# A three-stage kernel on one core: list masks from 16-bit pairs, softmax sums in groups of five tiles, V spread on GpSimd

## The chip, the cores and the metric

The kernel runs on one core of one Trainium2 chip. The metric is the device time of one execution in microseconds. Five engines work beside each other, each through its own queue in order: TensorE (PE; its weight loads are listed as PEld), VectorE (DVE), ScalarE (ACT), GpSimd (POOL) and SyncE (SP, which only issues transfers).

## The reference, cut to what matters

Three stages follow each other: attention over pooled keys and values, a mixture of experts with the best two of eight, and a dense two-layer block.

```
# attention: B, H, S, D = 8, 8, 576, 64; keys and values are means over 8 rows
k_p = k.reshape(B, H, Sp, 8, D).mean(axis=3);  v_p = v.reshape(B, H, Sp, 8, D).mean(axis=3)
scores = 1/sqrt(D) * q @ k_p.T
attn = exp(scores - max);  attn /= attn.sum + 1e-9
x = (attn @ v_p).transpose(0, 2, 1, 3).reshape(4608, 512)
# experts: N, D, E, F = 4608, 512, 8, 1024
logits = x @ w_gate + log1p(exp(x @ w_noise)) * noise
top2 = the two largest of 8;  w = softmax over the two
out[t] = sum over its two experts of w * (relu(x[t] @ w1[e]) @ w2[e])
# dense block: 512 -> 2048 -> 512
h = x @ w_in;  result = (h - tanh(h)) @ w_out
```

## The kernel before, in words

**Attention** (function attention) walks over 36 tiles of 128 tokens. It is a software pipeline written out by hand: in step t of one loop the exponentials of tile t stand beside the matmuls of its neighbours. In the order of one step: ACT does the exponentials of tile t (st_exps) and copies x transposed of tile t-4 (st_xT); DVE does the softmax sum of tile t-1 (st_norm: add 1e-9, reciprocal) and the scaled output of tile t-6 (st_g: the rows xr, which go to memory, and the gate logits lg); PE transposes the attention weights of tile t-2 (st_attT) and q of tile t+2 (st_q), multiplies the scores of tile t+1 (st_scores, after which DVE takes the row maximum mx), multiplies the output of tile t-5 with the identity and the gate weights (st_x, into px, of which there is one buffer), and attention weights by V of tile t-3 (st_av). px of one tile can be written only when xr and lg of the tile before have been read out of it.

Each of the 8 batches (4.5 tiles) has its K and V loaded, summed over the 8 rows of a pool in three halvings (the first on GpSimd for batches from 2 on, five instructions each for K and V; the other two on VectorE), and spread. For V this is vscale: VectorE computes a power of two from the largest value (lines 101 to 103), a scaled mask of8 (L1261), and in one instruction of 1280 elements per partition VB, the V of all heads set apart from each other (L1262). VB has two buffers, for even and odd batches. st_av of the batch's first tile stands one step later.

**The gate** (gate_jobs, lists) works on groups of 10, 10, 9 and 7 tiles as soon as their logits are there. It is a Python generator: each yield is a place where the loop may go on with other work. tick(n) takes n such pieces; a step of the loop has a fixed number of ticks, between its own instructions, so that the gate's small VectorE instructions stand spread between those of attention. What PE has to multiply is held until the next tick_pe. After the last tile, six more steps empty the pipeline (a step then ends in eight ticks), and what is left of the gate is taken in the first units of the first expert.

The lists say which tokens go to which expert's slot. For up to five tiles at a time, lists builds 0/1 masks and multiplies them on PE: l_one is 1 where the slot number k (of 80) equals a token's column, l_col holds that mask times the tile's first token number (head) and, by ACT, times the lane; l_row is 1 where k (of 128) equals a token's row. Before, l_one and l_col are one VectorE instruction of 800 elements each (L1465, L1466), and l_row is one instruction of 256 elements per tile (L1470), each with its own tick. Columns, rows and head are 32-bit numbers with one value per token, read with a stride of zero; the slot numbers and the masks are 16-bit.

**Experts and dense block.** When the second group is done, its lists give the tokens of expert 0's first 512 rows, which POOL gathers (L1587) and PE transposes (L1598). moe then runs 24 groups of tokens through two matmul layers (L355 to L357, L377 to L379), in single 16-bit halves; the dense block follows. PSUM of attention is given back before the experts' first product (L355) starts.

Of the kernel before, what the change touches and what calls it, by code (L numbers as in the profile page):

```python
# [10 lines left out]
F32 = mybir.dt.float32  # L11
F16 = mybir.dt.float16
BF16 = mybir.dt.bfloat16
I32 = mybir.dt.int32
# [1095 lines left out]
def attention(nc, tc, st, V):  # L1110
# [104 lines left out]
    nz = ep.tile([128, NT, E], F32, name="nz")  # L1215
    for c in each:
        add(nc.vector, 0, "k", 4, slice(*c))
    head = ep.tile([128, NT], F32, name="head")
    nc.gpsimd.iota(head, pattern=[[128, NT]], base=0, channel_multiplier=0, allow_small_or_imprecise_dtypes=True)
    zero8 = ep.tile([128, 1, E], F32, name="zero8")  # L1220
    nc.vector.memset(zero8, 0.0)
    dd = ep.tile([128, NT], F32, name="dd")
# [3 lines left out]
    def prep_jobs(b, first=False):  # L1226
        tl = {}
# [26 lines left out]
        def vscale():  # L1254
            p = ps.tile([128, 1], F32, name="pt", bufs=4)
            nc.tensor.matmul(p, ones1, tl["vx"], start=True, stop=True)
            yield
            m = wk.tile([128, 3], F32, name="vs")
            pow2(nc, m, p)
            of8 = wk.tile([128, 5, 4], F32, name="of8")  # L1260
            ts(of8, of, m[:, 2:3], None, op0=OP.mult)  # L1261
            tt(VB[b % 2].rearrange("p c (j d) -> p c j d", d=D), tl["va"][:, :, 0:1].to_broadcast([128, 5, 4, D]),  # L1262
               of8[:, :, :, None].to_broadcast([128, 5, 4, D]), op=OP.mult)
            lo, hi = b * S, b * S + S
            t0, t1 = lo // 128, -(-hi // 128)
            for t in range(t0, t1):
                o0, o1 = max(lo - 128 * t, 0), min(hi - 128 * t, 128)
                if o1 - o0 < 128:
                    ts(isc[o0:o1, t:t + 1], m[o0:o1, 1:2], 1.0 / 128, None, op0=OP.mult)
            f0, f1 = -(-lo // 128), hi // 128  # L1270
            ts(isc[:, f0:f1], m[:, 1:2].to_broadcast([128, f1 - f0]), 1.0 / 128, None, op0=OP.mult)
# [35 lines left out]

    def st_exps(t):
        at = wk.tile([128, 2, 4, SP], F32, name="at", bufs=3)
        sm = wk.tile([128, 2, 4], F32, name="sm", bufs=3)  # L1310
        AT[t], SM[t] = at, sm
        for g, (p, mx) in enumerate(SC.pop(t)):
            for j in range(4):
                nc.scalar.activation(at[:, g, j], p[:, j], AF.Exp, bias=mx[:, j:j + 1], accum_out=sm[:, g, j:j + 1])  # L1314

    def st_norm(t):
        sm = SM.pop(t)
        ts(sm, sm, 1e-9, None, op0=OP.add)
        tick()
        rc = RC[t] = wk.tile([128, H], F32, name="rc", bufs=7)  # L1320
        nc.vector.reciprocal(rc, sm.rearrange("p a b -> p (a b)"))
        tick()

    def st_attT(t):
# [67 lines left out]
    def gate_jobs(t0, n):  # L1392
# [5 lines left out]
        def T(nm, shp=None, d=F32):  # L1398
            tl[nm] = ep.tile([128, n] + (shp or [E]), d, name="g_" + nm, bufs=1)
            return tl[nm]  # L1400
# [40 lines left out]
            nc.vector.tensor_reduce(sp, tl["oh"], axis=AX.X, op=OP.add)  # L1441
        yield
        spf = sp.rearrange("p t a o -> p t (a o)")
        hi, row = T("hi", [2], I32), T("row", [2])
        yield ts(hi, spf, 7, None, op0=OP.logical_shift_right)
        yield stt(row, hi, -128.0, spf, op0=OP.mult, op1=OP.add)
        yield tt(tl["e"], tl["e"], hi, op=OP.add)
        over = T("ov", [2])
        yield ts(over, hi, float(NB), 1000.0, op0=OP.is_ge, op1=OP.mult)
        yield tt(tl["e"], tl["e"], over, op=OP.add)  # L1450
        yield from lists(t0, n, row, tl["e"])

    def lists(t0, n, row, col):


        K = E * NB
        flat = idx[:, :, 0:NB]
        for c0 in range(0, n, LT):
            m = min(LT, n - c0)
            R = ep.tile([128, LT, 2, 128], F16, name="l_row", bufs=1)[:, 0:m]  # L1460
            C0 = ep.tile([128, LT, 2, K], F16, name="l_one", bufs=1)[:, 0:m]
            C = ep.tile([128, LT, 2, 2, K], F16, name="l_col", bufs=1)[:, 0:m]
            b = lambda a, k: a[:, c0:c0 + m, :, None].to_broadcast([128, m, 2, k])
            w = lambda k: slot[:, None, None, 0:k].to_broadcast([128, m, 2, k])
            yield tt(C0, w(K), b(col, K), op=OP.is_equal)  # L1465
            tt(C[:, :, :, 1], C0, head[:, t0 + c0:t0 + c0 + m, None, None].to_broadcast([128, m, 2, K]),  # L1466
                                    op=OP.mult)
            yield nc.scalar.activation(C[:, :, :, 0], C0, AF.Copy, scale=lane)
            for j in range(m):
                yield tt(R[:, j], w(128)[:, j], b(row, 128)[:, j], op=OP.is_equal)  # L1470
            yield "pe"
            p = gate_ps[-1]([128, 2, E, NB])
            for j in range(m):
                for a in range(2):
                    nc.tensor.matmul(p.rearrange("p x e c -> p (x e c)"), R[:, j, a], C[:, j, a].rearrange("p x k -> p (x k)"),
                                     start=(j + a == 0), stop=(j == m - 1 and a == 1))
            yield 2 * (now[0] < NT)
            yield tt(flat, p[:, 0], flat, op=OP.add)
            yield tt(flat, p[:, 1], flat, op=OP.add)
# [241 lines left out]
```

## Time and profile before

| what | value |
|---|---|
| time, median of 3 runs | 1829.58 us (1828.01 to 1830.68) |
| the profiled execution | 1828.06 us, span 1826.2 us |
| PE busy in the span | 1763.6 us (97%) |
| DVE, ACT, POOL busy | 1301.2, 940.9, 263.2 us |
| mean granted clock of TensorE | 0.992 |

The profile's second part cuts the span into 40 slices of 45.7 us and gives the busy share of each engine in tenths. Attention takes the first six. From slice 7 on PE stands at 9 nearly throughout; in slices 1 and 4 to 6 it stands at 7 to 8, and the granted clock (PEclk) falls to 8 in slice 6:

```
PE   7998889999999999999999999999999999999998
DVE  5788867776676667566566456687878879787775
PEclk8999989999999999999999999999999999999999
```

(The slices are counted from 1 here. The lines are those of the page.)

### The profile page before, as it was taken

The page shows a single profiled execution, that of the slowest core. Times are in us where ns is not written, and L with a number is a line of the kernel's source. Part 1 is how long each engine was busy: PE and PEld are TensorE (multiplying, and loading weights), DVE is VectorE, ACT ScalarE, POOL GpSimd, SP SyncE. Part 2 cuts the span into 40 slices and gives each one's busy share as a digit, 9 for nine tenths or more (in the row PEclk, how much of TensorE's full clock was granted, in tenths as well). Part 3 has the DMA queues.
Part 4 walks back from the last instruction along what each step waited for, and adds up shares of the span by engine and source line. Part 5 has one row for each costly group of instructions (what it writes and reads, how often), then busy time and mean ns, then how long its engine had stood idle before and what let it go on. Part 6 is the DMA issues. An engine that isn't in the chain of part 4 may idle for free. (4 is left out here: it accounts for less than half of the span.)

```text
span 1826.2 us, 28991 instructions
## 1 busy us (share of the span) xinstructions
PE 1763.6 (97%) x10791; PEld 1077.7 (59%) x10792; DVE 1301.2 (71%) x2640; ACT 940.9 (52%) x2249; POOL 263.2 (14%) x258
## 2 busy tenths in 40 slices
PE   7998889999999999999999999999999999999998
PEld 5998874445445454545445454566666666666664
DVE  5788867776676667566566456687878879787775
ACT  5886732443434343443424245565766657666554
POOL 2222001312113030110101012110111201010000
PEclk8999989999999999999999999999999999999999
DMA  9867223464464545454544434531313313041100
GB/s 224 236 166 205 61 74 108 141 161 130 141 187 122 183 129 165 139 147 124 146 106 121 103 110 120 118 89 34 93 38 74 83 42 91 24 93 46 37 24 25
DMA packets 264158, 203.45 MB, mean 111 GB/s; under 512 B 188160, under 2 KB 208640, under 8 KB 264000
## 3 DMA queue, kind: packets, MB, share of 16 engines
q1 hardware_dynamic: 251840, 162.16, 33.0%
q0 software_dynamic: 11904, 38.81, 8.2%
q8 instruction: 88, 1.44, 0.3%
q14 instruction: 70, 0.57, 0.1%
q10 hardware_dynamic: 256, 0.46, 0.1%
HBM read 121.82 MB, written 45.74 MB: 92 GB/s over the span
## 5 line engine op out<-in xcount | busy, mean ns | idle before, releaser
L359 ACT ACTIVATE hT<-ph 128x512 f16<-128x512 f32 (+2 forms) x192 | 96.8, 505 | 425.0 <-PE ph L357 418.8
L355 PE MATMUL ph<-xTp,pair 128*128 128x384 f16 (+2 forms) x736 | 245.2, 333 | 14.0 <-DMA xTp<-xp 4.8
L356 PE MATMUL ph<-xTp,pair 128*128 128x384 f16 (+2 forms) x736 | 244.9, 333 | 0.4 <-DVE xTp L336 0.4
L357 PE MATMUL ph<-xTp,pair 128*128 128x384 f16 (+2 forms) x736 | 244.9, 333 | 0.0
L360 DVE SCALAR_TENSOR_TENSOR hT<-ph,hT 128x512 f16<-128x512 f32 (+2 forms) x192 | 110.8, 577 | 163.3 <-ACT hT L359 161.5
L1042 PE MATMUL py<-wo,gT 128*128 128x512 f16 x576 | 218.3, 379 | 1.0 <-issue 1.0
L1040 PE MATMUL py<-wo,gT 128*128 128x512 f16 x576 | 218.3, 379 | 0.1
L377 PE MATMUL py<-pair,hT 128*128 128x512 f16 x576 | 218.3, 379 | 0.0
L378 PE MATMUL py<-pair,hT 128*128 128x512 f16 x576 | 218.3, 379 | 0.0
L379 PE MATMUL py<-pair,hT 128*128 128x512 f16 x576 | 218.3, 379 | 0.0
L1041 PE MATMUL py<-wo,gT 128*128 128x512 f16 x576 | 218.3, 379 | 0.0
L899 PEld LDWEIGHTS <-wi 128*128 128x128 f16 x1536 | 150.3, 98 | 58.5 <-issue 0.2
L315 POOL DMA_INDIRECT xg<-x_d,idx x75 | 85.5, 1139 | 669.8 <-DVE xp L342 462.3
L713 POOL DMA_INDIRECT y<-y_d,ridx x64 | 78.9, 1233 | 518.5 <-DVE y L724 240.7
L355 PEld LDWEIGHTS <-pair 128*128 128x128 f16 x768 | 75.0, 98 | 83.6 <-issue 24.9
L356 PEld LDWEIGHTS <-pair 128*128 128x128 f16 x768 | 75.1, 98 | 61.8 <-issue 6.0
L357 PEld LDWEIGHTS <-pair 128*128 128x128 f16 x768 | 75.1, 98 | 57.1 <-issue 0.6
L999 ACT ACTIVATE th<-th,bias 128x512 f32<-128x512 f32 x144 | 102.5, 712 | 3.3 <-DVE th L997 1.6
L1000 DVE SCALAR_TENSOR_TENSOR th<-th,t 128x512 f32<-128x512 f32 x144 | 98.6, 684 | 1.4 <-ACT th L999 1.4
L989 DVE TENSOR_TENSOR gT<-th,gT 128x512 f16<-128x512 f32 x144 | 98.7, 685 | 0.2 <-ACT gT L988 0.2
L996 DVE SCALAR_TENSOR_TENSOR t<-hb,cinf,hs 128x512 f32<-128x512 f32 x64 | 48.0, 749 | 70.9 <-ACT hs L995 68.8
L1314 ACT ACTIVATE at<-psc,mx 128x72 f32<-128x72 f32 x288 | 87.8, 334 | 18.6 <-DVE mx L1303 18.6
(305 smaller groups left out, 3496.6 us busy)
## 6 DMA issues: line engine op xcount, KB each, us to landing
stage<-in_moe_w SPq DMA_DIRECT2D x64, 512.0 KB
y_d<-ys SPq DMA_DIRECT2D x82, 256.0 KB
x_d<-xr SPq DMA_DIRECT2D x36, 256.0 KB
out<-o SPq DMA_DIRECT2D x36, 256.0 KB
qt<-in_q SPq DMA_DIRECT2D x32, 256.0 KB
raw<-in_moe_w_in SPq DMA_DIRECT2D x32, 256.0 KB
raw<-in_moe_w_out SPq DMA_DIRECT2D x32, 256.0 KB
kt<-in_k SPq DMA_DIRECT2D x7, 768.0 KB
```

What stands on the lines that cost most here:

```text
L355: nc.tensor.matmul(p[:, :nt], w[:, 0, m, s], x[:, 0, m, :nt], start=(m == 0), stop=False)
L356: nc.tensor.matmul(p[:, :nt], w[:, 0, m, s], x[:, 1, m, :nt], start=False, stop=False)
L357: nc.tensor.matmul(p[:, :nt], w[:, 1, m, s], x[:, 0, m, :nt], start=False, stop=(m == KD - 1))
L360: stt(h[:, 1, :nt], p[:, :nt], 0.0, h[:, 0, :nt], op0=OP.max, op1=OP.subtract)
L377: nc.tensor.matmul(p, h[:, 0, s], w[:, 0, f], start=(f == 0), stop=False)
L378: nc.tensor.matmul(p, h[:, 0, s], w[:, 1, f], start=False, stop=False)
L379: nc.tensor.matmul(p, h[:, 1, s], w[:, 0, f], start=False, stop=(f == KF - 1))
L899: nc.tensor.matmul(p, w[:, a, m], y[:, c, b, m], start=(start and m + x == 0), stop=(m == 1 and x == 2), skip_group_check=True)
L999: nc.scalar.activation(q, q, AF.Square, bias=bias[:, 2:3], scale=SP5)
L1040: nc.tensor.matmul(p, g[:, 0, s], wo[:, 0, f], start=(f == 0), stop=False)
L1041: nc.tensor.matmul(p, g[:, 0, s], wo[:, 1, f], start=False, stop=False)
L1042: nc.tensor.matmul(p, g[:, 1, s], wo[:, 0, f], start=False, stop=(f == KF - 1))
```

## The change

Four things are changed, all in attention.

- **Masks in pairs.** row, col and head become 16-bit, and each value is stored twice side by side (a last dimension of 2). The three mask operations read pairs, so that every operand of theirs is 16-bit with two neighbours in its innermost dimension. The sum e + over is written straight into the pairs of col.
- **Row masks as one operation.** l_row of up to five tiles is one instruction of 1280 elements, and so one tick where there were five.
- **Softmax sums per five tiles.** The exponentials' sums are gathered for five tiles (the groups that the tuple sums marks: five tiles, twice four or less). The addition of 1e-9 and the reciprocal are done once for the group, after its last tile; in the other steps their two ticks are taken without them.
- **V on GpSimd.** For batches from 2 on, the instruction that writes VB is issued on GpSimd. For batches 0 and 1 it stays on VectorE.

```diff
@@ -1215,8 +1215,8 @@
     nz = ep.tile([128, NT, E], F32, name="nz")
     for c in each:
         add(nc.vector, 0, "k", 4, slice(*c))
-    head = ep.tile([128, NT], F32, name="head")
-    nc.gpsimd.iota(head, pattern=[[128, NT]], base=0, channel_multiplier=0, allow_small_or_imprecise_dtypes=True)
+    head = ep.tile([128, NT, 2, 2], F16, name="head")
+    nc.gpsimd.iota(head, pattern=[[128, NT], [0, 4]], base=0, channel_multiplier=0, allow_small_or_imprecise_dtypes=True)
     zero8 = ep.tile([128, 1, E], F32, name="zero8")
     nc.vector.memset(zero8, 0.0)
     dd = ep.tile([128, NT], F32, name="dd")
@@ -1259,7 +1259,7 @@
             pow2(nc, m, p)
             of8 = wk.tile([128, 5, 4], F32, name="of8")
             ts(of8, of, m[:, 2:3], None, op0=OP.mult)
-            tt(VB[b % 2].rearrange("p c (j d) -> p c j d", d=D), tl["va"][:, :, 0:1].to_broadcast([128, 5, 4, D]),
+            (nc.gpsimd if b > 1 else nc.vector).tensor_tensor(VB[b % 2].rearrange("p c (j d) -> p c j d", d=D), tl["va"][:, :, 0:1].to_broadcast([128, 5, 4, D]),
                of8[:, :, :, None].to_broadcast([128, 5, 4, D]), op=OP.mult)
             lo, hi = b * S, b * S + S
             t0, t1 = lo // 128, -(-hi // 128)
@@ -1307,18 +1307,28 @@
 
     def st_exps(t):
         at = wk.tile([128, 2, 4, SP], F32, name="at", bufs=3)
-        sm = wk.tile([128, 2, 4], F32, name="sm", bufs=3)
-        AT[t], SM[t] = at, sm
+        if t in sums:
+            SM[0] = wk.tile([128, 5, 2, 4], F32, name="sm"), t
+        sm, t0 = SM[0]
+        AT[t] = at
         for g, (p, mx) in enumerate(SC.pop(t)):
             for j in range(4):
-                nc.scalar.activation(at[:, g, j], p[:, j], AF.Exp, bias=mx[:, j:j + 1], accum_out=sm[:, g, j:j + 1])
+                nc.scalar.activation(at[:, g, j], p[:, j], AF.Exp, bias=mx[:, j:j + 1], accum_out=sm[:, t - t0, g, j:j + 1])
+        if t + 1 in sums or t + 1 == NT:
+            SM[1] = sm, t0
 
     def st_norm(t):
-        sm = SM.pop(t)
+        if not (t + 1 in sums or t + 1 == NT):
+            tick(2)
+            return
+        sm, t0 = SM.pop(1)
+        sm = sm[:, 0:t + 1 - t0]
         ts(sm, sm, 1e-9, None, op0=OP.add)
         tick()
-        rc = RC[t] = wk.tile([128, H], F32, name="rc", bufs=7)
-        nc.vector.reciprocal(rc, sm.rearrange("p a b -> p (a b)"))
+        rc = wk.tile([128, 5, H], F32, name="rc")[:, 0:t + 1 - t0]
+        nc.vector.reciprocal(rc, sm.rearrange("p t a b -> p t (a b)"))
+        for u in range(t0, t + 1):
+            RC[u] = rc[:, u - t0]
         tick()
 
     def st_attT(t):
@@ -1441,14 +1451,15 @@
             nc.vector.tensor_reduce(sp, tl["oh"], axis=AX.X, op=OP.add)
         yield
         spf = sp.rearrange("p t a o -> p t (a o)")
-        hi, row = T("hi", [2], I32), T("row", [2])
+        hi, row, col = T("hi", [2], I32), T("row", [2, 2], F16), T("col", [2, 2], F16)
+        two = lambda a: a[:, :, :, None].to_broadcast([128, n, 2, 2])
         yield ts(hi, spf, 7, None, op0=OP.logical_shift_right)
-        yield stt(row, hi, -128.0, spf, op0=OP.mult, op1=OP.add)
+        yield stt(row, two(hi), -128.0, two(spf), op0=OP.mult, op1=OP.add)
         yield tt(tl["e"], tl["e"], hi, op=OP.add)
         over = T("ov", [2])
         yield ts(over, hi, float(NB), 1000.0, op0=OP.is_ge, op1=OP.mult)
-        yield tt(tl["e"], tl["e"], over, op=OP.add)
-        yield from lists(t0, n, row, tl["e"])
+        yield tt(col, two(tl["e"]), two(over), op=OP.add)
+        yield from lists(t0, n, row, col)
 
     def lists(t0, n, row, col):
 
@@ -1460,14 +1471,13 @@
             R = ep.tile([128, LT, 2, 128], F16, name="l_row", bufs=1)[:, 0:m]
             C0 = ep.tile([128, LT, 2, K], F16, name="l_one", bufs=1)[:, 0:m]
             C = ep.tile([128, LT, 2, 2, K], F16, name="l_col", bufs=1)[:, 0:m]
-            b = lambda a, k: a[:, c0:c0 + m, :, None].to_broadcast([128, m, 2, k])
-            w = lambda k: slot[:, None, None, 0:k].to_broadcast([128, m, 2, k])
-            yield tt(C0, w(K), b(col, K), op=OP.is_equal)
-            tt(C[:, :, :, 1], C0, head[:, t0 + c0:t0 + c0 + m, None, None].to_broadcast([128, m, 2, K]),
-                                    op=OP.mult)
+            g = lambda a: a.rearrange("p t a (k i) -> p (t a) k i", i=2)
+            b = lambda a, t, k: a[:, t:t + m].rearrange("p t a i -> p (t a) i")[:, :, None].to_broadcast([128, 2 * m, k // 2, 2])
+            w = lambda k: slot[:, None, 0:k].to_broadcast([128, 2 * m, k]).rearrange("p m (k i) -> p m k i", i=2)
+            yield tt(g(C0), w(K), b(col, c0, K), op=OP.is_equal)
+            tt(g(C[:, :, :, 1]), g(C0), b(head, t0 + c0, K), op=OP.mult)
             yield nc.scalar.activation(C[:, :, :, 0], C0, AF.Copy, scale=lane)
-            for j in range(m):
-                yield tt(R[:, j], w(128)[:, j], b(row, 128)[:, j], op=OP.is_equal)
+            yield tt(g(R), w(128), b(row, c0, 128), op=OP.is_equal)
             yield "pe"
             p = gate_ps[-1]([128, 2, E, NB])
             for j in range(m):
```

How the instructions stand now is shown at three places. The first is VectorE's queue where the V of batch 4 is spread, in the steps in which the first group's lists begin; of is the scaled mask, vs the power of two, isc its inverse, g_e, g_hi, g_ov and g_col the lists' column numbers. Before:

```order
L1261 TENSOR_SCALAR of_1803<-of,vs 128x20
L1262 TENSOR_TENSOR vb_155<-vt_111,of_1803 128x1280
L1269 TENSOR_SCALAR isc<-vs 64x1
L1271 TENSOR_SCALAR isc<-vs 128x4
L1447 TENSOR_TENSOR g_e<-g_e,g_hi 128x20
L1318 TENSOR_SCALAR sm<-sm 128x8
L1449 TENSOR_SCALAR g_ov<-g_hi 128x20
L1321 RECIPROCAL rc<-sm 128x8
L1450 TENSOR_TENSOR g_e<-g_e,g_ov 128x20
L1368 TENSOR_TENSOR xr<-px,rc 128x512
L1374 TENSOR_TENSOR lg<-px,rc 128x128
```

And of the change, the same place:

```order
L1261 TENSOR_SCALAR of_1740<-of,vs 128x20
L1269 TENSOR_SCALAR isc<-vs 64x1
L1271 TENSOR_SCALAR isc<-vs 128x4
L1458 TENSOR_TENSOR g_e<-g_e,g_hi 128x20
L1460 TENSOR_SCALAR g_ov<-g_hi 128x20
L1461 TENSOR_TENSOR g_col<-g_e,g_ov 128x40
L1378 TENSOR_TENSOR xr<-px,rc 128x512
L1384 TENSOR_TENSOR lg<-px,rc 128x128
L1477 TENSOR_TENSOR l_one<-slot,g_col 128x800
L1478 TENSOR_TENSOR l_col<-l_one,head 128x10x80
```

VB has left the queue, and so have the sum and the reciprocal of a single tile; the two instructions of the output, xr and lg, now have five instructions between themselves and the mask (L1261), where they had eight.

The second place is GpSimd's queue from the load of batch 2 on: kt and vt are the first halvings of K and V (five instructions in a row each), x the gather for expert 0. Before:

```order
L1141 TENSOR_TENSOR vt_112<-vt_112 128x256 x5
L1141 TENSOR_TENSOR kt_109<-kt_109 128x256 x5
L1141 TENSOR_TENSOR vt_111<-vt_111 128x256 x5
L1141 TENSOR_TENSOR kt_110<-kt_110 128x256 x5
L1141 TENSOR_TENSOR vt_112<-vt_112 128x256 x5
L1587 DMA x_3092<-x_d,i_3040 128x512
```

And of the change, the same stretch of the queue:

```order
L1262 TENSOR_TENSOR vb_155<-vt_111,of_1740 128x1280
L1141 TENSOR_TENSOR kt_109<-kt_109 128x256 x5
L1141 TENSOR_TENSOR vt_111<-vt_111 128x256 x5
L1262 TENSOR_TENSOR vb_156<-vt_112,of_2062 128x1280
L1141 TENSOR_TENSOR kt_110<-kt_110 128x256 x5
L1141 TENSOR_TENSOR vt_112<-vt_112 128x256 x5
L1262 TENSOR_TENSOR vb_155<-vt_111,of_2465 128x1280
L1262 TENSOR_TENSOR vb_156<-vt_112,of_2793 128x1280
L1597 DMA x_2880<-x_d,i_2811 128x512
```

Each VB stands behind the V additions of the next batch and ahead of the K additions of the one after; the last two stand ahead of the gathers.

The third place is VectorE's queue in the steps that empty the pipeline, where the lists of the third group are made while the last tiles' outputs are read out (x0T is expert 0's first input, lz the group's logits, idx the lists). Before:

```order
L1465 TENSOR_TENSOR l_one<-slot,g_e 128x800
L1466 TENSOR_TENSOR l_col<-l_one,head 128x10x80
L1470 TENSOR_TENSOR l_row<-slot,g_row 128x256
L1368 TENSOR_TENSOR xr<-px,rc 128x512
L1374 TENSOR_TENSOR lg<-px,rc 128x128
L1470 TENSOR_TENSOR l_row<-slot,g_row 128x256 x4
L1601 TENSOR_TENSOR x0T<-pt,x0T 128x4x128 x2
L1368 TENSOR_TENSOR xr<-px,rc 128x512
L1374 TENSOR_TENSOR lg<-px,rc 128x128
L1376 TENSOR_REDUCE lz<-lg 128x32
L1478 TENSOR_TENSOR idx<-pt,idx 128x8x10
L1479 TENSOR_TENSOR idx<-pt,idx 128x8x10
```

And of the change, from the same list block on:

```order
L1477 TENSOR_TENSOR l_one<-slot,g_col 128x800
L1478 TENSOR_TENSOR l_col<-l_one,head 128x10x80
L1480 TENSOR_TENSOR l_row<-slot,g_row 128x1280
L1611 TENSOR_TENSOR x0T<-pt,x0T 128x4x128 x2
L1378 TENSOR_TENSOR xr<-px,rc 128x512
L1384 TENSOR_TENSOR lg<-px,rc 128x128
L1386 TENSOR_REDUCE lz<-lg 128x80
L1378 TENSOR_TENSOR xr<-px,rc 128x512
L1384 TENSOR_TENSOR lg<-px,rc 128x128
L1488 TENSOR_TENSOR idx<-pt,idx 128x8x10
L1489 TENSOR_TENSOR idx<-pt,idx 128x8x10
L1477 TENSOR_TENSOR l_one<-slot,g_col 128x640
```

The list block now comes with three tiles' outputs still to be read out behind it, where there were two: the gate has moved one step ahead, since a block of five tiles takes four ticks fewer.

## Rows read from the trace of the kernel before

**Rows 1.** The page, first part: busy us (share of the span) and instructions of each engine.

```profile
PE 1763.6 (97%) x10791; PEld 1077.7 (59%) x10792; DVE 1301.2 (71%) x2640; ACT 940.9 (52%) x2249; POOL 263.2 (14%) x258
```

**Rows 2.** Busy time by stretch: us, PE, PEld, DVE, ACT, POOL (instructions), PEclk, DMA share, GB/s.

```profile
107.00:222.00 115.00, 103.18 (x861) 97.09 (x859) 99.55 (x271) 87.13 (x377) 20.76 (x25) 0.99 0.53 143
222.00:236.00 14.00, 11.70 (x62) 11.71 (x63) 6.38 (x24) 3.99 (x20) 1.12 (x1) 0.63 0.11 39
...
245.20:265.40 20.20, 12.65 (x100) 11.39 (x99) 16.52 (x43) 4.55 (x8) 1.90 (x2) 0.92 0.23 75
265.40:310.00 44.60, 42.36 (x214) 19.59 (x215) 33.92 (x113) 9.93 (x17) 3.06 (x3) 1.00 0.33 108
310.00:1826.20 1516.20, 1488.75 (x8776) 845.51 (x8773) 1065.07 (x1984) 754.31 (x1471) 204.79 (x173) 1.00 0.38 102
```

**Rows 3.** Waits of PE from 107 to 266: us in total, times, longest.

```profile
PE px L1357 <- DVE lg L1374: 14.6, 7, 4.3
PE ph L355 <- DVE idx L1479: 1.6, 1, 1.6
```

**Rows 4.** PE in order of time: start us, us, operation, count, [idle before and its releaser].

```profile
138.16 1.95 PE L1344 MATMUL pt<-aT,vb 128*128 128x128 f32 x16
...
145.77 1.32 PE L1357 MATMUL px<-wgn,xT 128*128 128x160 f32 x8 [3.25 <-DVE lg L1374]
146.93 3.48 PE L1344 MATMUL pt<-aT,vb 128*128 128x128 f32 x16
...
169.09 3.68 PE L1344 MATMUL pt<-aT,vb 128*128 128x64 f32 x32
...
224.30 1.32 PE L1357 MATMUL px<-wgn,xT 128*128 128x160 f32 x8 [2.49 <-DVE lg L1374]
225.46 6.79 PE L1344 MATMUL pt<-aT,vb 128*128 128x64 f32 x32
...
252.69 1.32 PE L1357 MATMUL px<-wgn,xT 128*128 128x160 f32 x8 [1.70 <-DVE lg L1374]
...
258.80 1.58 PE L1357 MATMUL px<-wgn,xT 128*128 128x160 f32 x8 [4.29 <-DVE lg L1374]
...
265.42 0.38 PE L355 MATMUL ph<-x0T,pair 128*128 128x512 f16 x1 [1.59 <-DVE idx L1479]
```

**Rows 5.** VectorE instructions by line and shape, 0 to 340: busy us, mean ns.

```profile
L1470 DVE TENSOR_TENSOR l_row<-slot,g_row 128x256 f16<-128x256 f16 x36 | 14.9, 443 | 0.0
L1262 DVE TENSOR_TENSOR vb<-vt,of 128x1280 f32<-128x1280 f32 x8 | 11.9, 1492 | 0.3
L1318 DVE TENSOR_SCALAR sm<-sm 128x8 f32<-128x8 f32 x36 | 7.9, 220 | 0.0
L1321 DVE RECIPROCAL rc<-sm 128x8 f32<-128x8 f32 x36 | 7.2, 200 | 0.8
L1465 DVE TENSOR_TENSOR l_one<-slot,g_e 128x800 f16<-128x800 f16 x6 | 5.9, 986 | 0.1
L240 DVE TENSOR_SCALAR cb<-raw 128x256 int32<-128x256 int32 x8 | 2.4, 294 | 0.0
L1465 DVE TENSOR_TENSOR l_one<-slot,g_e 128x640 f16<-128x640 f16 x1 | 0.8, 815 | 0.0
```

**Rows 6.** VectorE in order of time, start us, us: a reciprocal of 36, batch 4's VB.

```profile
304.01 0.38 DVE L1693 RECIPROCAL coef<-coef 128x36 f32<-128x36 f32 x1
...
133.97 1.49 DVE L1262 TENSOR_TENSOR vb<-vt,of 128x1280 f32<-128x1280 f32 x1
```

**Rows 7.** VectorE and POOL in order of time: the same instruction beside POOL and alone.

```profile
143.42 4.55 POOL L1141 TENSOR_TENSOR vt<-vt 128x256 f32<-128x256 f32 x5 [9.55 <-DMA vt<-in_v]
143.74 0.69 DVE L1318 TENSOR_SCALAR sm<-sm 128x8 f32<-128x8 f32 x1
...
171.03 0.16 DVE L1318 TENSOR_SCALAR sm<-sm 128x8 f32<-128x8 f32 x1
```

**Rows 8.** POOL instructions by line and shape, 0 to 340: busy us, mean ns.

```profile
L1141 POOL TENSOR_TENSOR vt<-vt 128x256 f32<-128x256 f32 x30 | 23.0, 798 | 60.0 <-DMA vt<-in_v 30.5 <-DVE lg L1374 12.1 <-DVE kt L1141 9.3
```

## The prediction

> **What bounds the kernel now.** First the busy shares: PE has 97% of the span, no other engine over 71% [rows 1], so time can be won only where PE loses it. The table by stretch says where that is: from 310 us on PE is busy 1488.75 of 1516.2 us at full clock, and the little it loses there lies in code that the change does not touch. In the loop of attention (107 to 222 us) it loses 11.8 of 115 us, and VectorE is busy 99.55 of these: about as full as PE [rows 2]. From 222 to 236 PE loses 2.3 us, and its granted clock is 0.63 of full speed. From 245.2 to 265.4, while the pipeline empties, it is idle for 7.55 of 20.2 us, and VectorE is busy 16.5.
>
> Then the waits of PE: the largest is px behind lg, 14.6 us in seven waits [rows 3]. There is one px; the next tile's product waits until VectorE has read xr and lg out of it, and VectorE comes late because the lists, the gate, the weights' preparation and K and V stand ahead in its queue. In order of time, last, one sees what a wait costs besides itself: behind waits of 3.25 and 2.49 us the same matmuls run at the lower clock level (1.2 in place of 2.4 GHz), st_av taking 3.48 in place of 1.95 us, and a split tile's 6.79 in place of 3.68. Behind a wait of 1.70 they don't [rows 2, 4]. So the bound of this part is VectorE's queue, and the metric follows it through px.
>
> **Masks.** One block of five tiles now takes two instructions of 800 at 0.986 us (l_col is l_one's equal in size) and five of 256 at 0.443: 4.19 us. The rows of 800 and 640 elements differ by 0.171 us for 160: 1.07 ns for an element and 0.13 us fixed [rows 5]. After the change there are two of 800 and one of 1280. Upper end: no faster rate, 0.99 + 0.99 + 1.49 (VB has 1280 elements [rows 5]) = 3.47, a saving of 0.72. Lower end: two elements in the time of one, 0.56 + 0.56 + 0.81 = 1.93, a saving of 2.26. Which holds no row shows for two tensors; the nearest is L240, a VectorE instruction with one tensor and 256 elements in 0.294 us, against 0.443 for l_row's 256 [rows 5], so the engine has a faster rate for operands of one kind. I take the lower end, 2.26 for a block of five, with four chances in five. The Trainium skill, "VectorE: DVE Perf Modes", section on the perf-mode tier table, says that an operation on two tensors runs at twice the rate when all operands are 16-bit with neighbours adjacent and in SBUF, and at the single rate for 32-bit ones; no run here shows it yet, and by it a block saves the same 2.26.
>
> Row, col and head become a few dozen elements longer: under 0.03 us for an instruction at 1.07 ns for an element, nothing.
>
> **Softmax sums.** 36 additions at 0.220 and 36 reciprocals at 0.200 [rows 5] become eight of each with up to 40 elements. The nearest row for that size is a reciprocal of 36, 0.38 us [rows 6]; between 0.20 and 0.38 for each of the two, I take 0.35. In the loop's stretch (18 tiles, four groups) that is 7.6 removed and 2.8 added, 4.8 us less. Nothing comes late by it: the first reader of a group is xr of its first tile, a step behind the group's sum in the same queue.
>
> **V on GpSimd.** Six instructions of 1.49 us leave VectorE [rows 5], four in the loop's stretch: 6.0 us. On POOL the nearest row is the additions, 0.798 us for 256 elements [rows 8]; five of them have VB's 1280 elements and take 4.0, or 4.55 in the row with VectorE busy beside them [rows 7]. Below, 1.49 is the end. I take 3.5, that is 4.0 less four starts of 0.13. Two things hang on it.
>
> First, st_av. VB of batch 4 starts at 133.97 and the first st_av that reads it at 138.16 [rows 4, 6]: 4.2 us, in which 3.5 fit. Ahead of VB in POOL's queue stand the V additions of the next batch, due a step earlier; behind it the K additions of the one after, which are not read for more than a step. So no wait on PE is counted.
>
> Second, VectorE itself. While POOL adds, the sum's addition takes 0.69 in place of 0.16 us on VectorE [rows 7]: it stands still until POOL's instruction is over. One long instruction on POOL can then hold up VectorE for as long as it lasts, from the first instruction on that is so affected. By the order, that is the third behind the mask for batch 4 (g_e) and batch 5 (the sums), but the fourth or later for 3, 6 and 7, behind xr and lg, which read PSUM, or the weights' small ones; for batch 2 nothing of the kind comes in time. I estimate 3, 3, 1 and 2 us for batches 4 to 7: 9 us of standing still for 6.0 removed, so this part costs VectorE 3 us in the loop. Between the ends (no hold-up, 6.0 saved; four full hold-ups of 4.55, 12 lost) this is near the middle. The Trainium skill, "SBUF — State Buffer", section "Who interferes with whom", has the rule: a VectorE instruction with two SBUF inputs, or in a mode that uses both ports, and a GpSimd one shut each other out for the whole instruction. The 0.69 above agrees with it; by it the move alone would slow the kernel.
>
> **The sum.** In the loop's stretch VectorE gets lighter by 4 × 2.26 + 4.8 − 3 = 10.8 us of 99.55. PE loses 11.8 there; it can't win all, since the first lists and batch 4's VB fall into one step, where the hold-up stands against the saving. I take 8 (between 5 and 11).
>
> From 222 to 236, 11.7 us of PE work at a clock of 0.63 are 7.4 at full speed: 6.6 us are lost, all behind the wait of 2.49 [rows 2, 4]. The second group's lists are then already done, and that wait gets shorter by about 1.5 us, below the 1.70 that kept its clock. The step falls or stays as a whole: 4.5 is the mean that I take (0 to 6.6).
>
> In the emptying of the pipeline VectorE loses a block of five (2.26) and one of four (4 × 0.443 + 2 × 0.815 = 3.4, to 1.6: 1.8 less); by the order the lists are also begun one step ahead. That makes 4 from the work and up to 7.55 from what PE loses: I take 5.
>
> From 265.4 to 310 PE loses 2.2 us [rows 2]. The last group's gate starts earlier, but its nine steps now stand together ahead of the second unit's hT, so a wait for its mask of about 2 us replaces what goes: 0, from −2 to +2.
>
> In all 17.5 us. Behind 310 nothing can absorb it, PE being busy to 98%. The profiled execution took 1828.06 us, so 1810.6; the median of the runs is 1.5 higher: **1812 us**.
>
> **Rivals.**
> - *GpSimd holds up VectorE more than that.* VB takes 4.5 us or more, and all four hold-ups are full: 12 us lost in place of 3, and the loop's gain falls to about 2, that of the slow-clock stretch to about 2. Then 1829.6 − 9 = 1821. For it: every VB has two inputs in SBUF read with strides of zero, of which no row of POOL tells. Against: only some instructions are affected.
> - *The masks stay at the single rate.* A block saves 0.72 in place of 2.26: 6 us less in the loop, 3 in the emptying: a gain of 8.5, 1821.
> - *The lost time was PE's anyway.* Other waits (ACT's copies, scores) take the place of lg; a gain of under 3: 1828. Against: the next largest wait is 1.6 against 14.6 [rows 3].
> - *Everything is won:* 11.8 + 6.6 + 7.55 and 2 of the experts' start, 28: 1802. For it, VB without a hold-up.
> - *Slower: V comes too late.* One mechanism at one place: VB ends after st_av wants to start. From about 4 us on POOL the PE stalls, and from 6.7 us the stall exceeds 2.49, behind which the clock fell. With a VB of 8 us the stalls are 6 × 3.8 = 23, the slow clock adds some 2 each, 12, and the masks' and sums' gain of 20 does not cover it: 1829.6 + 15 = 1845. Against: 0.798 us for 256 elements.
>
> **How the numbers follow.** The forecast has a chance of 0.62, with a range of its own from 1806 to 1818. GpSimd's hold-up 0.11, single rate 0.08, everything won 0.07, PE's own 0.07, V too late 0.05. From 1801 to 1825 lie the forecast, the two smaller gains and most of the full one, over 0.8. A measurement of this kernel can tell 0.2%, 3.7 us, from no change. Faster by more: 0.62 + 0.11 + 0.08 + 0.07 = 0.88, less 0.01 for a hold-up at its worst: 0.87. Within: 0.07. Slower: 0.06.
>
> **What would show it.** In the profile after: l_one and l_col at 0.56 us and l_row at 0.81 for 1280 (at 0.99 and 1.49 the single rate holds); additions and reciprocals of the sums eight times each, at 0.3 to 0.4; POOL's VB near 3.5, and behind it VectorE instructions of small size that take 2 to 3 us; px waiting for lg for less than 7 us in all; the clock of 222 to 236 at 1.0. Wrong it would be made by a PE wait for VB at st_av, or by waits on px as long as now although VectorE's work is less.

## The result: 1809.3 us, and the profile after

The changed kernel takes 1809.34 us (median of five runs, 1807.22 to 1810.30) against 1829.58: a ratio of 0.9891, with an interval from 0.9875 to 0.9908. The forecast was 1812, its own range 1806 to 1818.

The page's busy line and four stretches of the changed kernel answer to [rows 1, 2] (same columns). The last two stretches are the first 45 us of the experts and what follows:

```profile
PE 1754.3 (97%) x10791; PEld 1069.2 (59%) x10792; DVE 1282.7 (71%) x2550; ACT 940.8 (52%) x2249; POOL 277.6 (15%) x264
...
107.00:222.00 115.00, 107.66 (x919) 101.67 (x918) 97.26 (x249) 91.16 (x397) 31.51 (x33) 1.00 0.55 153
222.00:236.00 14.00, 12.66 (x111) 11.53 (x109) 9.46 (x30) 6.96 (x14) 1.89 (x2) 1.00 0.26 77
...
249.00:294.00 45.00, 43.35 (x218) 20.35 (x219) 28.49 (x101) 8.98 (x16) 3.05 (x3) 1.00 0.31 109
294.00:1807.60 1513.60, 1485.99 (x8764) 844.41 (x8762) 1065.12 (x1984) 754.55 (x1471) 206.06 (x173) 1.00 0.38 103
```

In the loop PE now loses 7.3 us where it lost 11.8, and from 222 to 236 its clock is 1.00 where it was 0.63. VectorE's 97.26 us in the loop can't be set against the 99.55 of before: the new kernel does more in these 115 us (919 matmuls for 861). So compare the same 17 tiles, from the px product near 113 us to the one that starts at 224.30 before and at 216.37 now (same columns, first before, then the new kernel):

```profile
112.95:224.30 111.35, 97.23 (x809) 91.17 (x808) 97.87 (x263) 82.44 (x357) 20.23 (x25) 0.98 0.49 133
```

```profile
112.98:216.37 103.39, 96.05 (x819) 90.06 (x818) 88.95 (x222) 83.24 (x359) 28.84 (x29) 1.00 0.52 143
```

Over these tiles VectorE is 8.9 us lighter and the stretch 8.0 shorter. From the totals alone it would seem that PE gets nearly every microsecond that VectorE is spared; the experiments show that it does not.

PE's waits from 107 to 250, then PE in order of time (columns as in [rows 3, 4]):

```profile
PE px L1367 <- DVE lg L1384: 5.7, 4, 2.5
PE pt L1342 <- ACT xT L1360: 1.4, 2, 1.1
```

```profile
68.14 1.25 PE L1367 MATMUL px<-wgn,xT 128*128 128x160 f32 x8
...
144.92 1.35 PE L1367 MATMUL px<-wgn,xT 128*128 128x160 f32 x8 [0.80 <-DVE lg L1384]
...
216.37 1.32 PE L1367 MATMUL px<-wgn,xT 128*128 128x160 f32 x8 [1.43 <-DVE lg L1384]
217.53 3.68 PE L1354 MATMUL pt<-aT,vb 128*128 128x64 f32 x32
...
222.69 1.95 PE L1354 MATMUL pt<-aT,vb 128*128 128x128 f32 x16
...
242.98 1.32 PE L1367 MATMUL px<-wgn,xT 128*128 128x160 f32 x8 [2.47 <-DVE lg L1384]
...
249.07 0.39 PE L355 MATMUL ph<-x0T,pair 128*128 128x512 f16 x1 [0.62 <-DVE idx L1489]
```

The waits for lg fall from 14.6 to 5.7 us. Against [rows 4] the second split tile's st_av starts 7.9 us earlier (217.53 for 225.46) and takes 3.68 in place of 6.79; the experts' first product, L355, starts 16.35 earlier (249.07 for 265.42). The next group shows VectorE by line and shape (columns as in [rows 5], 0 to 340 us), the last two rows in order of time, uncontended:

```profile
L1271 DVE TENSOR_SCALAR isc<-vs 128x4 f32<-128x4 f32 x8 | 7.7, 964 | 0.1
L1480 DVE TENSOR_TENSOR l_row<-slot,g_row 128x1280 f16<-128x1280 f16 x6 | 5.1, 844 | 0.0
L1477 DVE TENSOR_TENSOR l_one<-slot,g_col 128x800 f16<-128x800 f16 x6 | 4.4, 726 | 0.1
L1329 DVE RECIPROCAL rc<-sm 128x40 f32<-128x40 f32 x6 | 2.4, 402 | 0.2
L1326 DVE TENSOR_SCALAR sm<-sm 128x40 f32<-128x40 f32 x6 | 1.6, 260 | 0.0
```

```profile
196.78 0.57 DVE L1477 TENSOR_TENSOR l_one<-slot,g_col 128x800 f16<-128x800 f16 x1
...
198.24 0.82 DVE L1480 TENSOR_TENSOR l_row<-slot,g_row 128x1280 f16<-128x1280 f16 x1
```

The masks run at 0.57 and 0.82 us where nothing holds them (forecast 0.56 and 0.81). And isc, four elements, has a mean of 0.964 us, which the forecast did not have.

### The profile page after: what moved, and what is told of

Read it like the earlier page. It is cut to its first block, busy times and chain, and to the rows that moved or that the text cites. A ratio compares the mean times of both kernels' runs of the same rounds, so it can differ in the third digit from the quotient of the medians.

```text
span 1807.6 us, 28937 instructions
## 1 busy us (share of the span) xinstructions
PE 1754.3 (97%) x10791; PEld 1069.2 (59%) x10792; DVE 1282.7 (71%) x2550; ACT 940.8 (52%) x2249; POOL 277.6 (15%) x264
## 5 line engine op out<-in xcount | busy, mean ns | idle before, releaser
L355 PE MATMUL ph<-xTp,pair 128*128 128x384 f16 (+2 forms) x736 | 245.2, 333 | 15.0 <-DMA xTp<-xp 6.0
L355 PEld LDWEIGHTS <-pair 128*128 128x128 f16 x768 | 75.0, 98 | 83.0 <-issue 23.2
L1042 PEld LDWEIGHTS <-gT 128*128 128x128 f16 x576 | 56.3, 98 | 69.3 <-DVE gT L989 1.5
```

The source lines that it names most:

```text
L355: nc.tensor.matmul(p[:, :nt], w[:, 0, m, s], x[:, 0, m, :nt], start=(m == 0), stop=False)
L1042: nc.tensor.matmul(p, g[:, 1, s], wo[:, 0, f], start=False, stop=(f == KF - 1))
```

## The experiments

**The measure.** Beside the time, each run is read by T, the stretch from the px product near 68 us to the first L355. T is 197.27 us before (265.42 less 68.15) and 180.93 after, and 197.66 and 180.68 in the second profiles (e3, e10). The table also has what the lower clock (granted 0.5 of full speed) takes within T: 1 less the granted clock, times T. In the kernel before that is 8.5 us, half of the time by which the change shortens T. A fall of the clock can come or stay away behind the same wait (shown at the end), and one that takes 1.7 us stands in e1, e4, e6 and e11 and not in the new kernel, e2 or e12. So only between runs with the same clock are differences from about 0.5 us on told; else less than 2 us says nothing of the edit. The rest of the span, behind L355, is 1558 to 1568 us over all profiles, and 1560.8 and 1568.4 for the kernel before alone; a small difference in time can therefore not be assigned without T.

| kernel | T, us | T less the new one's 180.8 | lower clock in T: us | px behind lg, 90 to 300: us | ratio of times |
|---|---|---|---|---|---|
| before (and e3) | 197.3, 197.7 | 16.7 | 8.5, 8.5 | 14.6, 14.1 | 1, 0.9996 |
| new (and e10) | 180.9, 180.7 | 0 | 0, 0 | 5.7, 5.7 | 0.9891, 0.9905 |
| e1 V back | 181.7 | 0.9 | 1.7 | 4.7 | 0.9901 |
| e2 sums back | 181.3 | 0.5 | 0 | 6.5 | 0.9900 |
| e4 V in five pieces | 180.3 | -0.5 | 1.7 | 4.2 | 0.9906 |
| e5 old masks | 195.3 | 14.5 | 6.8 | 13.2 | 0.9995 |
| e6 new masks alone | 181.7 | 0.9 | 1.7 | 5.3 | 0.9920 |
| e7 masks in 32 bits | 187.5 | 6.7 | 3.4 | 6.1 | 0.9953 |
| e8 rows apart | 186.3 | 5.5 | 3.4 | 10.7 | 0.9932 |
| e9 dose | 191.6 | 10.8 | 8.5 | 8.8 | (one run, 1821.85 us) |
| e11 low late | 180.4 | -0.4 | 1.7 | 5.2 | 0.9912 |
| e12 and isc first | 179.0 | -1.8 | 0 | 4.4 | 0.9911 |

The intervals of the ratios are 0.0012 to 0.0021 to either side, so the times alone don't tell the ratios of 0.989 to 0.992 apart.

**e1: V back on VectorE.**

```
- (nc.gpsimd if b > 1 else nc.vector).tensor_tensor(VB[b % 2]...
+ tt(VB[b % 2]...
```

> The new kernel with the spreading of V back on VectorE in all eight batches; masks and sums stay new. Theory (the prediction's): moving V won nothing, because GpSimd's instruction of 2.33 us holds a small VectorE instruction up for as long as it lasts. VectorE gets 6 x 1.49 = 8.9 us back and is rid of 3 held isc (6.5 us), one held g_col (2.0) and some slowing of list masks. So the time stays within 3 us of the new kernel's 1809.3: 1806 to 1812, L1271 takes 0.15 us each time, px waits for lg 5 to 7 us. Rival 1: the move won its full 1.49 us a batch, the hold-ups falling where VectorE had room: 1813 to 1817. Rival 2: the hold-ups fall at the places that PE waits for: 1802 to 1806.

1810.97 us, T 0.9 us longer, isc 0.16 us again. The waits at 144.9 and 216.4 (0.80 and 1.43) become 0.18 and 0.78. A little later PE waits for the lists (idx) where the new kernel waits 1.12 us for ScalarE's xT, and behind this wait the clock fell (0.91 from 140 to 160):

```profile
149.97 0.63 PE L1342 MATMUL pt<-identf,at 128*96 128x128 f32 x2 [1.38 <-DVE idx L1489]
```

The fall alone can make up the 0.9 us, so neither a gain nor a loss by moving V is shown. The theory (that it won nothing) stands.

**e2: sums for each tile again.**

```
- if not (t + 1 in sums or t + 1 == NT): ... (one of each for up to five tiles)
+ ts(sm, sm, 1e-9, None, op0=OP.add); nc.vector.reciprocal(rc, sm...)   # every tile
```

> The new kernel with one addition and one reciprocal of the sums for each tile again; masks and V stay new. Theory: VectorE gets 18 x 0.42 less 4 x 0.66 = 4.9 us more in the loop, and some of it is lost at px, as PE now waits only 5.7 us there: 1811 to 1815. Rival: VectorE has room now and the sums are hidden: 1808 to 1810.5.

1811.25 us, the lower end of the theory's range; T 0.5 us longer, which T can just tell, with the clock up throughout in both. Over the same tiles VectorE is 2.1 us busier (91.06 for 88.95), not the 4.9 expected, and the stretch is as long as in the new kernel (103.40 for 103.39): the rival was nearer.

**e3: meant as the old masks.**

> The new kernel with the old masks (one operation for each tile's row mask, operands in the old layout); sums and V stay new. Theory: the masks are the largest part, 2.2 us for each block of five, 1.8 for the block of four, and with them the low clock behind a wait over 2.4 us comes back: 1819 to 1826, clock under 0.9 in at least one 10-us slice after 130 us. Rival: sums and V alone have given VectorE enough room: 1811 to 1816, clock at 1.0.

What ran was, by a slip in the edit, the kernel before itself (1829.41 us, T 197.66). It says nothing on the masks and serves as the repeat of before; e5 is the run that was meant.

**e4: V in five pieces on GpSimd** (`for c in range(5): ...tensor_tensor(VB[b % 2][:, c]...`; the first two batches, on VectorE, are cut up too).

> The new kernel with GpSimd's spreading of V cut into five instructions of 256 elements each (the first two batches on VectorE too). Theory: VectorE and GpSimd shut each other out for one instruction at a time, so no VectorE instruction is held longer than one piece: isc and g_col take at most 0.7 us in place of 2.3, GpSimd's five pieces take 3.0 to 3.6 us in all, and a wait of PE of that size goes: 1806 to 1809. Rival: the hold-up is no matter of the instruction's length (isc still 2 us or more), or the pieces hold up more VectorE instructions each a little: 1809 to 1812.

isc has a mean of 0.32 us in place of 0.96, g_col 0.35 in place of 1.21: the hold-up is as long as GpSimd's instruction. The pieces take 0.64 us each, 2.9 to 3.6 a batch. T is 0.5 shorter although the clock fell once (behind px at 242.70). The time, 1813.66, is above both expected ranges, and its ratio (0.9906) can't be told from the new kernel's: no gain in time is shown.

**e5: the old masks, sums and V new** (head, row and col in 32 bits, `b` and `w` as before, five `l_row` instructions with a tick each).

> The new kernel with the old masks (32-bit list numbers, one row mask for each tile); sums and V stay new. With V back the experts' first product (L355) started 0.6 us later than in the new kernel (249.1), with the old sums 1.2 us later; before, it starts at 265.4. Theory A (the masks carry it, sums and V help only a little beside them): first product at 260 to 265, 1821 to 1828 us, px waits for lg 11 us or more. Theory B (any of the three parts gives VectorE most of the room, so one can be left out): 251 to 257, 1811 to 1817.

1829.93 us, slightly above theory A's range: without the masks nothing is left in the time, and in T some 2 us, of which the lower clock can make up 1.7. PE in order of time shows why (one wait of the kernel before, then e5):

```profile
161.88 1.35 PE L1357 MATMUL px<-wgn,xT 128*128 128x160 f32 x8 [1.74 <-DVE lg L1374]
```

```profile
147.34 2.47 PE L1367 MATMUL px<-wgn,xT 128*128 128x160 f32 x8 [3.86 <-DVE lg L1384]
...
225.01 2.47 PE L1367 MATMUL px<-wgn,xT 128*128 128x160 f32 x8 [3.33 <-DVE lg L1384]
```

The wait of 1.74 us at 161.88 is gone, but those of 3.25 and 2.49 [rows 4] have grown to 3.86 and 3.33. Ahead of the second, in the same step as a block of masks, isc stands for 2.33 us, held up by GpSimd's VB. That this is where the spared time of sums and V comes back is argued from the rows, not tested. Theory A stands.

**e6: the new masks alone.**

> The kernel before with the new masks alone. Theory A: first product at 250 to 254, 1810 to 1815 us. Theory B: 255 to 260, 1816 to 1821.

1815.34 us, slightly above theory A's range, T 181.7: 15.8 us of the 16.7 come with the masks alone, and the clock's one fall can account for the rest. Of the time the masks' share is less sharp (0.9920 with 0.9900 to 0.9941).

**e7: the same mask instructions, operands in 32 bits** (`head`, `row` and `col` as F32).

> The new kernel with the same mask instructions in the same order, but row, col and head in 32 bits: this tells the rate of the masks from their number and order. Theory A (rate): l_one and l_col take 0.98 us again and l_row 1.45 to 1.5, a block of five 3.4 in place of 1.95; px waits for lg 8 to 12 us, the first product at 254 to 259, 1814 to 1820 us. Theory C (the gain comes from the four fewer instructions and ticks of a block, by which the lists run a step earlier): 249 to 251, 1809 to 1812.

1821.81 us, T 6.7 us longer. By line and shape in e7, then PE's two largest waits from 107 to 258 and the first product that waits for l_row:

```profile
L1480 DVE TENSOR_TENSOR l_row<-slot,g_row 128x1280 f16<-128x1280 f16 x6 | 9.1, 1510 | 0.0
L1477 DVE TENSOR_TENSOR l_one<-slot,g_col 128x800 f16<-128x800 f16 x6 | 6.4, 1061 | 0.1
```

```profile
PE px L1367 <- DVE lg L1384: 6.1, 3, 3.7
PE pt L1485 <- DVE l_row L1480: 3.4, 4, 1.5
```

```profile
143.19 0.86 PE L1485 MATMUL pt<-l_col,l_row 128*128 128x160 f16 x10 [1.54 <-DVE l_row L1480]
```

One 32-bit operand of three puts the whole instruction back to the single rate: 1.51 in place of 0.82. The rule of the Trainium skill that the prediction weighed agrees with both: "VectorE: DVE Perf Modes", section "What auto-detection actually checks", lets the doubled rate for packed 16-bit elements come in if every tensor is 16-bit. The rate is worth 6.7 us of the 14.5, not all; theory A's time was exceeded by 2 us. One expectation failed: px was to wait 8 to 12 us for lg and waits 6.1, hardly more than in the new kernel (5.7). What grows is PE's wait for the masks themselves, 3.4 us in place of 0.5, and the lower clock, 3.4 us. So px is the largest place where PE depends on VectorE, but not the only one.

**e8: five row masks with a tick each, at the new rate** (`for j in range(m): yield tt(g(R)[:, 2 * j:2 * j + 2], ...`).

> The new kernel with the row mask as five instructions of 256 elements again, each with its tick, at the new 16-bit layout: number and order of before at the new rate. A piece takes 0.23 to 0.27 us, a block of five 2.3 to 2.5 in place of 1.95. Theory A: first product at 249.5 to 252, 1809 to 1813 us. Theory C: 254 or later, 1815 or more.

1818.11 us, T 5.5 us longer: theory C was right here, and A wrong. VectorE in order of time, first the new kernel, then e8, at the first group's first block:

```profile
139.23 0.98 DVE L1480 TENSOR_TENSOR l_row<-slot,g_row 128x1280 f16<-128x1280 f16 x1
140.13 0.44 DVE L1303 TENSOR_REDUCE mx<-psc 128x4 f32<-128x288 f32 x1
140.50 1.38 DVE L159 SCALAR_TENSOR_TENSOR pair<-stage,wsc,pair 128x1024 f16<-128x1024 f32 x1
141.80 1.75 DVE L1141 TENSOR_TENSOR vt<-vt 128x640 f32<-128x640 f32 x2
143.58 0.49 DVE L1245 TENSOR_REDUCE vm<-vt 128x1 f32<-128x320 f32 x1
143.99 0.68 DVE L1378 TENSOR_TENSOR xr<-px,rc 128x512 f32<-128x512 f32 x1
```

```profile
141.40 0.65 DVE L1481 TENSOR_TENSOR l_row<-slot,g_row 128x256 f16<-128x256 f16 x2
141.97 1.27 DVE L159 SCALAR_TENSOR_TENSOR pair<-stage,wsc,pair 128x1024 f16<-128x1024 f32 x1
143.17 1.34 DVE L1141 TENSOR_TENSOR vt<-vt 128x640 f32<-128x640 f32 x2
144.54 0.48 DVE L1245 TENSOR_REDUCE vm<-vt 128x1 f32<-128x320 f32 x1
144.95 1.49 DVE L1481 TENSOR_TENSOR l_row<-slot,g_row 128x256 f16<-128x256 f16 x2
146.36 0.68 DVE L1378 TENSOR_TENSOR xr<-px,rc 128x512 f32<-128x512 f32 x1
```

With one instruction the block is done before the step's large jobs (L159, vt, vm). In five, the last two fall behind these jobs, straight ahead of xr, and there GpSimd's V additions (from 144.83) stretch each of them to 0.74 us; px then waits 3.26 us, as before the change. It is the order that counts here, not the work: over the same tiles VectorE is only 0.5 us busier than in the new kernel (89.45 for 88.95), and T is 5.5 longer, 3.4 of it lower clock. Undone singly the two halves cost 6.7 and 5.5 us, together 14.5, more than their sum: each leaves room that the other needs.

**e9: VectorE work that nothing reads, at chosen steps.**

```
+ for t in (21, 23, 25, 29, 31, 32, 33, 33):
+     at(t, tt, dose, dose, dose, OP.add)      # 128 x 1024
```

> The new kernel with VectorE additions on 1024 elements that nothing reads (1.1 to 1.25 us each) put in at eight places: five in steps of the loop in which px starts 2 to 4 us after lg is done (px of the new kernel at 157.5, 169.8, 191.4, 203.1 and 210.4 us), one in the step whose px waits at 144.9, two in the step whose px waits at 216.4. Theory (VectorE's time counts only in the steps in which px starts right behind lg): no new wait over 0.3 us at the five, the wait of 0.80 becomes 1.9 to 2.1, that of 1.43 becomes 3.6 to 4.0, and behind the latter, longer than the 2.49 behind which the clock fell in the kernel before, st_av of the split tile takes over 4 us in place of 3.68. First product of the experts 3.5 to 9 us later than 249.1: 252.6 to 258. Rival (a us of VectorE counts everywhere alike, as the prediction's subtraction has it): waits of px grow at the five places too, together by 3 us or more, and the first product comes 8 us or more later with no low clock.

One addition takes 1.21 us. Where px had started about 2 us or more behind lg, it gets no wait: at the second place lg is done at 167.78 and px starts at 169.75 in the new kernel (1.97 later), in e9 at 170.15 and 170.98 (0.83 later, no wait). So at all five: from the px at 153.47 to that at 211.79, 6 us of VectorE's time cost PE 0.2. At the other two places (PE, e9):

```profile
145.89 1.35 PE L1367 MATMUL px<-wgn,xT 128*128 128x160 f32 x8 [1.54 <-DVE lg L1384]
...
220.18 2.47 PE L1367 MATMUL px<-wgn,xT 128*128 128x160 f32 x8 [3.83 <-DVE lg L1384]
222.44 6.93 PE L1354 MATMUL pt<-aT,vb 128*128 128x64 f32 x32
...
252.52 2.44 PE L1367 MATMUL px<-wgn,xT 128*128 128x160 f32 x8 [2.48 <-DVE lg L1384]
```

The waits grow by 0.74 and 2.40 us, 3.1 for 3.6 of work. Behind the longer one the clock falls to its lower level: px 2.47 for 1.32, st_av 6.93 for 3.68, attT and the next px slower too. By the starts of the px products this costs 5.7 in all. A second fall, behind 2.48 us at 252.52, costs 1.6. Together 3.1 + 0.2 + 5.7 + 1.6 = 10.6, by which T grew over the new kernel's 180.93 (the expectation's 9 was too low by the second fall). The theory stands, the rival falls, in one profiled run.

**e10 to e12: the new kernel once more, and two further edits.** e11 takes `c2.low` (L159) out of steps 37 and 38 and issues it behind the loop; e12 also works isc out ahead of `of8` and VB, and spreads the last batch's V on VectorE.

> The new kernel itself once more, so that the next two are compared with it on the same chip: ratio to the kernel before 0.988 to 0.990, first product at 248.5 to 250.

> The new kernel with two VectorE instructions of 1.28 us (L159, the low halves of two chunks of the first expert's second weight) taken from the last steps of the loop, where px waits 2.47 us behind VectorE, and put behind the loop, where VectorE is idle from 249.16 to 252.55. Theory: the wait of 2.47 falls to 1.0 to 1.4, the first product starts 1.2 to 2.6 us earlier, 246.5 to 248, and the time falls by as much. Rival: hT of the first expert comes late behind the two (a PE wait of 1 us or more after 250 us) and nothing is left of it.

> As the run before, and isc is worked out ahead of the spreading of V, and the last batch's V is spread by VectorE again. Theory (the hold-up takes the first instruction behind GpSimd's start that can be held, whichever it is): batch 3's isc takes 0.15 us in place of 2.31 with nothing held in its place, as xr and lg follow; batch 5's hold-up moves to the sums, batch 4's stays with the list numbers; in batch 7 the wait of 1.43 at 216.4 falls by 0.5 to 0.9. First product 0.5 to 1.2 us earlier than in the run before. Rival (it is isc itself that is slow beside GpSimd): nothing is held up any more in batches 3, 5 and 7.

1810.84, 1813.41 and 1812.00 us: no difference that the times can tell. In T e11 wins 0.4 us, a miss: the wait at 243 falls only from 2.48 to 1.97, because x0T (L1611) stands ahead of xr and waits for ScalarE, and in this run the clock fell behind it. That fall costs 1.2 us: from this px to L355 e11 takes 7.28 us and e12, behind the same wait, 6.10. e12 wins 1.8 us in T, with the clock up throughout as in the new kernel; the wait at 216 is 0.68 as expected, and isc takes 0.16 each time. Batch 5's sums, which the theory expected to be held in its place, were not: sm had run, and the reciprocal begun, just before GpSimd began (e12, both engines):

```profile
160.77 0.18 DVE L1326 TENSOR_SCALAR sm<-sm 128x40 f32<-128x40 f32 x1
160.98 0.40 DVE L1329 RECIPROCAL rc<-sm 128x40 f32<-128x40 f32 x1
...
161.00 2.33 POOL L1270 TENSOR_TENSOR vb<-vt,of 128x1280 f32<-128x1280 f32 x1 [13.18 <-DVE sm L1326]
```

Batch 4's g_col is still held there (mean of the two of its size 1.26 us), so it is not isc that is slow beside GpSimd, and that rival falls too.

## Why the prediction held, and which of its steps did not

- **The bound.** Right: PE's loss followed VectorE's queue through px, 14.6 us of waits to 5.7, and no other wait took its place (the next is 1.4). With the waits went the lower clock, 8.5 us to 0. The rival that the time was PE's anyway falls, and so does the one that everything is won, as 5.7 us of waits are left. It is not the whole bound, though: PE also waits for the masks (e7).
- **Masks.** Price right: 0.57 and 0.82 us, the single rate only with 32-bit operands (e7). But the forecast counted their time alone; that one row mask saves four ticks, it used only for the emptying. e8 puts the row masks' number and order at 5.5 us of T, beside 6.7 for the rate.
- **Sums.** The price of the new instructions is near: 0.40 + 0.26 for a group of five tiles against 0.70. What they spare is less than "4.8 us": 2.1 over the same tiles (e2). It fits that short instructions of VectorE overlap in the rows, so that one spared frees less than its own time: in e2 g_e starts at 134.69 and takes 0.17, and sm starts at 134.78. And PE gets little of it: e2 finds 0.5. This is the step that failed: **VectorE's lighter load was subtracted as one number, 10.8 us of 99.55, and PE was given 8 of it.** The number was near (8.9), the rule behind it was not: in e9 6 us of VectorE in steps where px starts well behind lg cost PE 0.2, and 3.6 us in steps without such room cost 3.1 and the clock. Of the 17 px products from 107 to 222 in the kernel before, 11 started 0.5 to 4.6 us after lg was done; that a saving of 0.42 in each of those steps is worth next to nothing follows from e9 and e2, but was not tried in the kernel before.
- **V on GpSimd.** VB takes 2.33 us, not 3.5, but within the bounds. The mechanism is right: g_col in batch 4 and isc in batches 5 and 7 are held 2.1 us each in the loop, 6.4 for 6.0 removed. The size is smaller than forecast: over the same tiles VectorE is busy 88.95 us with V on GpSimd and 88.34 with V back (e1), a net of −0.6 against −3; the rival of full hold-ups by a VB of 4.5 us falls. Which instructions are held was half wrong, since isc, the next in the queue, was passed over. Whether the move wins PE anything e1 doesn't tell. VectorE in order of time and POOL, batch 4:

```profile
133.77 2.34 POOL L1262 TENSOR_TENSOR vb<-vt,of 128x1280 f32<-128x1280 f32 x1 [18.05 <-DVE of L1261]
133.95 2.22 DVE L1461 TENSOR_TENSOR g_col<-g_e,g_ov 128x40 f16<-128x40 f32 x1
```

- **No wait at st_av.** Right: no wait of PE for VB is in the trace, and the slower rival has nothing for it.
- **The sum.** 8 for the loop was 6.9, up to the wait of px at 224.30 (PE is done ahead of it at 221.81 before, at 214.94 now). 4.5 for the slow stretch was 6.7: the wait is 1.1 shorter, and behind it 5.6 more are won, nearly all of it clock (the next tile's st_av, at full clock in both, moves from 236.22 to 222.69, 13.5 earlier). The forecast took the mean of a fall and none; it went as a whole. 5 for the emptying was 2.8: its waits of 1.70, 4.29 and 1.59 [rows 4] fell to 0.97, 2.47 and 0.62, 3.5 less, not the expected up to 7.55. Together 16.35 of the 17.5. The experts' start, put at 0, loses 1.7 us of PE's time where it lost 2.2. The span fell by 18.5; the other 2.2 us lie behind L355, where the kernel before alone varies by 7.6, so no cause is given for them. That the sum came so near is in part luck: the slow stretch gave more, loop and emptying less, and in the loop the masks alone give nearly all (e6), while the sums, which were credited with 4.8, give 0.5 and the masks' order got no credit.

## What to carry to other kernels

Before pricing relief for an engine that has to empty a buffer before another may fill it again (here VectorE and px), list for each step how long after the last read the next write starts: in e9 only steps with next to nothing between counted, and there both the work and the order of what stands ahead of the read count. Look also for the other results that the waiting engine needs (the masks in e7). An instruction moved to GpSimd isn't free for VectorE: look which instruction VectorE issues next (isc, issued behind VB, takes up to 2.33 us, and ahead of it 0.16 in e12). Where only late stages vary from run to run, a stretch between two landmarks tells what the total time can't, if the granted clock within it is read beside it.

## What the runs showed of the hardware that was not expected

- A VectorE instruction of four elements with one tensor input (isc, 0.15 us alone) takes 2.31 to 2.33 us when it starts behind GpSimd's VB; xr and lg, which read PSUM, run beside it at their usual 0.68 and 0.28. The Trainium skill, "SBUF — State Buffer", "Who interferes with whom", counts tensor_scalar among the operations that can take the shared ports and lets the later one wait for the whole instruction: the rows agree, and with pieces of 0.64 (e4) the wait shrinks with them.
- GpSimd spreads V, 1280 elements in one instruction, in 2.33 us, and in five of 256 in 2.9 to 3.6.
- The length of a wait does not settle the clock. Behind 2.47 and 2.48 us at the same place it stayed (the new kernel, e10) and fell (e4, e9); behind 1.38 us it fell (e1); and of two waits of 1.97 us one lost it. The rows are px and the list product behind it in e4, px in e11 and px in e12:

```profile
242.70 1.46 PE L1368 MATMUL px<-wgn,xT 128*128 128x160 f32 x8 [2.47 <-DVE lg L1385]
243.96 1.54 PE L1486 MATMUL pt<-l_col,l_row 128*128 128x160 f16 x10
```

```profile
242.93 1.53 PE L1367 MATMUL px<-wgn,xT 128*128 128x160 f32 x8 [1.97 <-DVE lg L1384]
```

```profile
242.81 1.32 PE L1367 MATMUL px<-wgn,xT 128*128 128x160 f32 x8 [1.97 <-DVE lg L1384]
```

The forecast's line between 1.70 and 2.49 was too sharp. What decides, no run here shows.
